# Channels 0 to 3 and 4 to 7 on the two partition halves, and how half two's first inverse is evacuated

## The chip, the cores and the metric

The kernel runs on one core of a Trainium2 chip. The metric is the device time of one execution in microseconds (us). Engines are named as in the profile: PE multiplies matrices (PEld is its weight load), ACT, DVE and POOL work elementwise, SP issues most transfers. PSUM is the memory that PE writes, 8 banks of 512 float32 columns on 128 partitions; SBUF is the memory that everything else is kept in.

## The reference, cut to what matters

The input is a sequence of 2048 tokens with 512 channels. Two layers follow one another, and each is a long convolution with a gate, then an MLP:

```python
def _A_ref(q, k, v, shift_k, ssm_k, ssm_D):
    # a causal convolution of four taps over k, times v
    kv = k_shift * v
    kv_f = rfft(kv padded to 2 * S)          # along the sequence, for each channel
    kf_f = rfft(ssm_k padded to 2 * S)
    y = irfft(kv_f * kf_f)[:S]               # a causal convolution as long as the sequence
    y = y + kv * ssm_D
    return q * y

def _B_ref(x, w1, b1, w2, b2):
    h = gelu(layernorm(x) @ w1 + b1)
    return h @ w2 + b2

x = A_q
x = x + _A_ref(layernorm(x), A_k, A_v, A_shift_k, A_ssm_k, A_ssm_D)
x = x + _B_ref(layernorm(x), B_w1, B_b1, B_w2, B_b2)
# and the same two lines once more, with the same A_k, A_v, A_ssm_k and weights
```

Since k, v and the filter are the same in both layers, the convolution's result y is computed once and used twice.

## The kernel before, in words

The sequence is cut into two halves of 1024 tokens. The output of half one needs the convolution of half one's input with half one of the filter. That of half two needs two products, which are added in the frequency domain. Each convolution is a transform in two stages, a product, and an inverse in two stages, all by matmuls:

- `stage1` (PE on line 557) transforms along 128 points, for eight groups of eight channels in one PSUM tile of two banks. Its evacuation (line 560) reads, for each of 128 places, eight elements 128 columns apart, and writes 1024 in a row.
- `stage2` (PE on line 569) transforms along the remaining 8 points with the table S2. Its output has on the partitions 8 channels of a group x 8 frequencies x real and imaginary part, and the order of the channels there is the order of S2's columns. In the kernel before, the even channels 0, 2, 4, 6 are on partitions 0 to 63 and the odd ones on 64 to 127. Its evacuation reads the tile as `[512,2],[32,16],[1,32]` (step and count, outermost first) and, for the input's transforms (line 730 for half one, line 788 for half two), writes `[32,2],[64,16],[1,32]`.
- `inverse1` (PE on line 674) inverts the 8 points with the table U. For half one (`split` false) a group of eight channels takes two matmuls of 128 rows and 128 columns, and the evacuation (lines 681 and 682) reads `[8,16],[128,8],[1,8]` and writes `[512,16],[8,8],[1,8]`. For half two (`split` true) each group takes, for each half of the partitions (`g` 0 and 1), two matmuls of 64 rows and 64 columns. Half `g` writes bank `g` of the tile: 16 blocks of 32 columns, four channels for each of eight groups in a block. Since U does not mix channels, only the columns of the four channels of that half are taken from it. The evacuation of such a tile (lines 678 and 679) is the one that the change edits. There are eight tiles.
- `inverse2` (PE on line 696) inverts the 128 points, and needs the evacuations of all eight tiles of `inverse1`. Its result is y, with the tokens on the partitions.

`evac` on line 473 is ACT's copy out of PSUM (line 474 is DVE's), so all these evacuations have the same line in the profile. `tt` on line 468 is DVE's elementwise operation.

After that come blocks of one to four tiles of 128 tokens, for each half and layer: statistics (lines 810 to 825), normalisation (835 on ACT, 836 on DVE), times y and added, statistics again and normalisation, a transpose (on PE, or by a DMA on line 879), the first MLP matmul (`m1`, PE on line 899, with the GELU on ACT, line 904), and the second (`m2`, PE on line 933, added by DVE on line 937).

The order of all operations over all engines is written out by hand (`SEQ`), and so is the engine of each operation that could run on ACT, DVE or POOL (`ENGS`) and the PSUM banks of each tile (`BANKS`). Neither reads the data or the layout. From the order, `arrange` and `sync` work out which waits are needed; an engine runs its own list strictly in order. Around the edited place PE has the eight `inverse1` groups of half two interleaved with MLP matmuls of half one: three groups, one more, six `m2` matmuls, four groups, eleven `m2` matmuls, and then `inverse2`. The eight tiles share three pairs of banks, in PE's order 2, 4, 6, 2, 4, 2, 6, 4 (the first bank of each pair), so a group waits until the earlier tile in its banks has been evacuated. All eight evacuations are on ACT, one behind the other, in the order of the groups except that the third and the fourth change places; behind them stands a normalisation (line 835) of a later block.

Of the kernel before, what the change touches and what calls it, by code (L numbers as in the profile page):

```python
# [349 lines left out]
def _tables():  # L350

    be = np.arange(128)[:, None]
    k1 = 2 * np.arange(128)[None, :]
    th = TWO_PI * be * (k1 + 0.5) / 256
    F = np.concatenate([np.cos(th), -np.sin(th)], 1)
    a = np.arange(8)
    k2 = np.arange(8)
    f = 2 * np.arange(128)[:, None] + 0.5 + 256 * k2[None, :]
    th = TWO_PI * a[:, None, None] * f[None] / 2048
    c, s = np.cos(th), np.sin(th)  # L360
    S2 = np.zeros((2, 8, 8, 128, 2, 8, 8))
    for d in range(8):
        S2[0, :, d, :, 0, :, d] = c
        S2[1, :, d, :, 0, :, d] = s
        S2[0, :, d, :, 1, :, d] = -s
        S2[1, :, d, :, 1, :, d] = c
    S2 = S2[..., [0, 2, 4, 6, 1, 3, 5, 7]].transpose(0, 1, 2, 3, 6, 5, 4).reshape(128, 128 * 128)
    ph = TWO_PI * k2[:, None] * a[None, :] / 8
    c, s = np.cos(ph), np.sin(ph)
    U = np.zeros((2, 8, 8, 2, 8, 2, 8))  # L370
    for d in range(8):
        U[0, :, d, 0, :, 0, d] = c
        U[1, :, d, 0, :, 0, d] = -c
        U[0, :, d, 0, :, 1, d] = s
        U[1, :, d, 0, :, 1, d] = -s
        U[0, :, d, 1, :, 0, d] = -s
        U[1, :, d, 1, :, 0, d] = -s
        U[0, :, d, 1, :, 1, d] = c
        U[1, :, d, 1, :, 1, d] = c
    U = U[:, :, [0, 2, 4, 6, 1, 3, 5, 7]].transpose(2, 1, 0, 3, 4, 5, 6).reshape(128, 256)  # L380
    t = 8 * np.arange(128)[None, :] + a[:, None]
    ps = TWO_PI * t[None] * (2 * np.arange(128)[:, None, None] + 0.5) / 2048
    T2 = np.stack([np.cos(ps), -np.sin(ps)], 2) / 1024
    T2 = T2.reshape(128, 2048)
    sg = np.where(np.arange(128)[:, None] % 2 == 0, -1.0, 1.0) * np.ones((1, 16))
    return F, S2, U, T2, sg

# [5 lines left out]
def bass_interleave_layers__ssm_conv_h3__mixer_channel_mlp__prompt_kernel(  # L393
# [7 lines left out]
    def A(p0, n, off, *dims):  # L401
        return bass.AP(ar, p0 * AR + off, [[AR, n]] + [list(d) for d in dims])
# [7 lines left out]
    def Q(tile, p0, n, off, *dims):  # L410
        return bass.AP(ps, p0 * 4096 + tile.base * 512 + off, [[4096, n]] + [list(d) for d in dims])
# [12 lines left out]
    def place(n):  # L424
        o = pos[0]
        pos[0] += -(-n // 16) * 16
        return o

    R_ID, R_F, R_SG, R_B1 = place(192), place(256), place(16), place(16)
    R_U, R_DG, R_TC, R_HALO = place(256), place(1024), place(16), place(16)  # L430
# [15 lines left out]
    assert M_SG + 1 <= NS  # L446

    F, S2, U, T2, sg = _tables()
    t_sm = nc.inline_tensor(_bf(np.concatenate([np.eye(128), np.eye(128)[:, :64] + np.eye(128)[:, 64:], F, sg, U, T2], 1)), name="tab_small")
    t_s2 = nc.inline_tensor(_bf(S2), name="tab_s2")  # L450
# [19 lines left out]
    def evac(engs, dst, src, durs, tile):  # L470
        def f(e):
            if e is nc.scalar:
                return e.activation(dst, src(), AF.Copy)  # L473
            return e.tensor_copy(dst, src())  # L474
        return P.op(engs, f, durs, writes=[dst], tile=tile)

    BOTH = (ACT, DVE)
    E1 = {ACT: 912.0, DVE: 1135.0}
# [28 lines left out]
    tl = Tile(2)  # L507
# [7 lines left out]
    tl = Tile(1)  # L515
# [8 lines left out]
    for i in range(4):  # L524
        o, t = A(0, 128, R_DG + i * 256, [64, 4], [1, 64]), A(0, 128, R_TC + 4 * i, [1, 4], [0, 64])
# [36 lines left out]
    def stage2(G, t):  # L562

        tl = Tile(2)
        ins = [(i, A(0, 128, R_S2 + (16 * t + i) * 128, [1, 128]), A(0, 128, G + (16 * t + i) * 8, [1024, 8], [1, 8])) for i in range(16)]

        def f(e):
            for i, w, m in ins:
                r = e.matmul(Q(tl, 0, 128, i // 8 * 512 + i % 8 * 4, [32, 16], [1, 4]), w, m, start=True, stop=True)  # L569
            return r  # L570
        P.op(PE, f, 16 * 30.0, reads=[x for y in ins for x in y[1:]], tile=tl)
        return tl
# [81 lines left out]
    def hap(r, t, d, g=None):  # L654
        return A(0, 128, r + 64 * t + (4096 * g if g else 0), [d, 2], [512, 16 if g is None else 8], [1, 64])

    def inverse1(p, q, Z, split):

        for j in range(8):
            tl = Tile(2)  # L660
            ins = []
            for i in range(8):
                dg = 8 * j + i
                for n, r in enumerate((p, q)):
                    o = r + (dg // 4) * 512 + dg % 4
                    if split:
                        for g in range(2):
                            ins.append((512 * g + 4 * i, n, A(64 * g, 64, o, [4, 128]), A(64 * g, 64, R_U + n * 128 + g, [8, 16], [2, 4])))
                    else:
                        ins.append((i * 128, n, A(0, 128, o, [4, 128]), A(0, 128, R_U + n * 128, [1, 128])))  # L670

            def f(e, ins=ins, tl=tl):
                for i, n, w, m in ins:
                    r = e.matmul(Q(tl, 0, 128, i, *([32, 16], [1, 4]) if split else ([1, 128],)), w, m, start=n == 0, stop=n == 1)  # L674
                return r
            P.op(PE, f, 32 * 18.0 if split else 16 * 56.0, reads=[x for y in ins for x in y[2:]], tile=tl)
            if split:
                evac(BOTH, A(0, 128, Z + 64 * j, [1, 2], [512, 16], [2, 32]),
                     lambda tl=tl: Q(tl, 0, 128, 0, [512, 2], [32, 16], [1, 32]), E1, tl)
                continue  # L680
            evac(BOTH, A(0, 128, Z + 64 * j, [512, 16], [8, 8], [1, 8]),
                 lambda tl=tl: Q(tl, 0, 128, 0, [8, 16], [128, 8], [1, 8]), E1, tl)
# [25 lines left out]
    for t in range(8):  # L708
        tl = stage2(R_2, t)
# [17 lines left out]
    for t in range(8):  # L727
        tl = stage2(R_3, t)
# [24 lines left out]

    P.tag = "i1_0"
    inverse1(R_1, R_2, R_3, False)
    P.tag = "i2_0"
    inverse2(R_3, R_YT[0])

    P.tag = "h2_1"
    for t in range(8):  # L760
        tl = stage2(R_G1, t)
        for g in range(2):
            w = 64 * t + 32 * g
            o, x = A(0, 128, R_3 + w, [512, 16], [1, 32]), A(0, 128, HI + w, [512, 16], [1, 32])
# [7 lines left out]
    for t in range(8):  # L772
        o = hap(R_3, t, D1)
# [10 lines left out]
    for t in range(8):  # L784
        P.tag = "x2_1"
        tl = stage2(R_6, t)
        xo = R_KT + 1024 * (t % 4)
        evac(BOTH, A(0, 128, xo, [32, 2], [64, 16], [1, 32]), lambda tl=tl: Q(tl, 0, 128, 0, [512, 2], [32, 16], [1, 32]), E1, tl)
        o, p = hap(HH, t, HI - HH), hap(R_3, t, D1)
        tt(o, A(0, 128, xo, [0, 2], [64, 16], [1, 64]), o, ALU.mult, 1137.0)  # L790
        P.tag = "sum"
        tt(o, o, p, ALU.add, 1137.0)
    P.tag = "i1_1"
    inverse1(HH, HI, R_Z1, True)
    P.tag = "i2_1"
    inverse2(R_Z1, R_YT[1])
# [50 lines left out]
    for half in range(2):  # L847
        HTS, XTS, W = R_HT[half], R_XT[half], (256, 512)[half]
        for i in range(2):
            o = A(96, 1, HTS[i] + 10 * W, [1, W])  # L850
            P.op(POOL, lambda e, o=o: e.memset(o, 1.0), 100.0 + W, writes=[o])
        for L in range(2):
            s0 = 0
            for n in BLOCKS[half][L]:
# [18 lines left out]
                for i, (xo, yo) in enumerate(sl):  # L873
# [8 lines left out]
                    tl = Tile(1)  # L882
# [9 lines left out]
                for fc in range(11):  # L892
                    rows = 128 if fc < 10 else 96
                    tl = Tile(1)
                    ins = [(A(0, 128, R_W1 + dk * 1376 + fc * 128, [1, rows]), A(0, 128, XTS[k] + dk * W, [1, w])) for dk in range(4)]
# [11 lines left out]
                for i, (xo, yo) in enumerate(sl):  # L907
                    P.tag = "m2"
                    s = ids[i]
                    tl = Tile(1)  # L910
                    ins = []
# [62 lines left out]
```

## Time and profile before

| | us |
|---|---|
| median of 3 runs | 240.69 |
| lowest and highest | 240.51, 241.71 |
| the profiled execution | 240.1 |
| its span, first to last instruction | 238.2 |
| PE, DVE, ACT busy | 223.9, 176.6, 163.5 |

A row of a timeline gives the start from the beginning of the span, the time that the row lasts, the engine, the line, the operation with its shapes and how many instructions are in it, and in brackets the idle time ahead of it with what ended it. A row of the chain of work that ended last gives the start, the time and what that time belongs to. A row of a line's own view gives the shortest, the median and the longest duration in ns, and the first and the last start. A row of busy times by stretches gives the stretch, its length, the busy time of each engine with its instructions, the granted clock and the share of DMA.

### The profile page before, as it was taken

What the parts mean: (1) busy time and instruction counts of PE and PEld (TensorE: products, weight loads), DVE (VectorE), ACT (ScalarE), POOL (GpSimd) and SP (SyncE); (2) the same over time, 40 slices, a digit from 0 to 9 for tenths busy, and PEclk for the clock granted to TensorE, in tenths of its full rate; (3) what the DMA queues carried; (4) which work ended last, traced back from release to release, by engine and by line L of the source; (5) the groups of instructions that cost most, each with busy time, mean ns of one, the idle gap of its engine ahead of it and who ended that gap; (6) DMA issues with size and microseconds to landing.
All of it is one profiled execution on the core that took longest, in us unless ns stands there. A gap on an engine that the chain in (4) does not pass through costs nothing.

```text
span 238.2 us, 6507 instructions
## 1 busy us (share of the span) xinstructions
PE 223.9 (94%) x2743; PEld 147.7 (62%) x2765; DVE 176.6 (74%) x353; ACT 163.5 (69%) x258; POOL 57.0 (24%) x122
## 2 busy tenths in 40 slices
PE   6998788998999999998997999999999999999995
PEld 2897577876868587666866474844444444444453
DVE  0479989999999999999999599783269577605013
ACT  2485889999886779998969998477017415752540
POOL 2421030316412229177004232203020302300000
PEclk9999999999999999999999999999999999999999
DMA  5999789979959240022500203501300050033002
GB/s 158 360 387 388 279 219 196 304 237 174 165 121 277 51 91 3 1 47 49 174 0 6 44 4 66 154 3 22 66 1 3 0 132 0 0 69 117 37 3 88
DMA packets 41113, 26.77 MB, mean 112 GB/s; under 512 B 23702, under 2 KB 33788, under 8 KB 41084
## 3 DMA queue, kind: packets, MB, share of 16 engines
q1 hardware_dynamic: 40786, 26.20, 40.9%
q8 instruction: 22, 0.36, 0.6%
q10 hardware_dynamic: 298, 0.16, 0.3%
q14 instruction: 7, 0.06, 0.1%
HBM read 15.07 MB, written 2.10 MB: 72 GB/s over the span
## 4 chain that ended last, share of the span: by engine, by line
PE 64%; ACT 15%; DVE 9%; POOL 5%; DMA 4%; issue 2%; SPq 1%; DVEq 0%; ACTq 0%
PE ps L899 28%; PE ps L933 24%; ACT ar L473 13%; DVE ar L468 3%; PE ps L557 3%; POOL sm L825 3%; DMA ar<-in_A_ssm_k_dram 3%; PE ps L674 2%; DVE sm L810 2%; DMA ar<-ar 2%; ACT ar L835 2%; PE ps L696 2%; DVE ar L620 1%; PE ps L922 1%; PE ps L642 1%
## 5 line engine op out<-in xcount | busy, mean ns | idle before, releaser
L904 ACT ACTIVATE ar<-ps,sm 128x256 bf16<-128x256 f32 (+5 forms) x143 | 65.1, 525 | 36.3 <-PE ps L899 35.8
L473 ACT ACTIVATE ar<-ps 128x1024 bf16<-128x1024 f32 (+3 forms) x77 | 73.1, 1039 | 14.2 <-PE ps L557 5.9
L899 PE MATMUL ps<-ar 128*128 128x256 bf16 (+5 forms) x568 | 80.4, 297 | 0.3
L933 PE MATMUL ps<-ar 128*128 128x512 bf16 (+1 forms) x324 | 75.9, 380 | 1.4 <-issue 0.8
L899 PEld LDWEIGHTS ps<-ar 128*128 128x128 bf16 (+1 forms) x572 | 52.5, 100 | 27.3 <-ACT ar L473 0.4
L468 DVE TENSOR_TENSOR ar<-ar 128x512 bf16<-128x512 bf16 (+3 forms) x105 | 62.9, 637 | 6.1 <-ACT ar L835 5.5
L933 PEld LDWEIGHTS ps<-ar 128*128 128x128 bf16 (+1 forms) x341 | 32.1, 98 | 35.5 <-ACT ar L904 0.6
L810 DVE BATCH_NORM_STATS2 sm<-ar 128x6 f32<-128x512 bf16 x64 | 42.5, 682 | 0.4
L835 ACT ACTIVATE ar<-ar,sm 128x512 bf16<-128x512 bf16 x37 | 28.4, 811 | 12.7 <-DVE sm L822 7.5
L815 POOL TENSOR_SCALAR sm<-sm 128x2 f32<-128x2 f32 (+2 forms) x23 | 7.4, 323 | 106.1 <-DVE sm L811 105.6
L937 DVE TENSOR_TENSOR ar<-ar,ps 128x512 bf16<-128x512 bf16 x31 | 20.5, 677 | 16.0 <-PE ps L933 16.0
L817 POOL TENSOR_TENSOR sm<-sm 128x2 f32<-128x2 f32 (+2 forms) x26 | 22.1, 851 | 18.5 <-DVE sm L815 16.6
L557 PE MATMUL ps<-ar 128*64 128x128 bf16 x512 | 18.4, 227 | 2.8 <-ACT ar L473 1.1
L569 PE MATMUL ps<-ar 128*128 128x64 bf16 x512 | 18.3, 194 | 1.2 <-ACT ar L473 1.0
L557 PEld LDWEIGHTS ps<-ar 128*64 128x64 bf16 x512 | 15.8, 115 | 5.6 <-issue 2.1
L569 PEld LDWEIGHTS ps<-ar 128*128 128x128 bf16 x512 | 16.9, 98 | 3.8 <-ACT ar L473 2.0
L825 POOL TENSOR_SCALAR sm<-sm 128x1 f32<-128x1 f32 x43 | 17.6, 424 | 2.0
L836 DVE TENSOR_SCALAR ar<-ar,sm 128x512 bf16<-128x512 bf16 x27 | 10.7, 407 | 7.5 <-POOL sm L825 7.3
L474 DVE CAST ar<-ps 128x1024 bf16<-128x1024 f32 x11 | 13.1, 1220 | 3.2 <-PE ps L569 1.9
L674 PE MATMUL ps<-ar 64*128 64x64 bf16 (+1 forms) x384 | 12.6, 203 | 1.5 <-ACT ar L473 1.1
L674 PEld LDWEIGHTS ps<-ar 64*128 64x128 bf16 (+1 forms) x384 | 11.9, 114 | 2.8 <-ACT ar L473 1.4
L474 DVE COPY ar<-ps 128x1024 bf16<-128x1024 bf16 (+1 forms) x9 | 5.5, 632 | 8.1 <-PE ps L520 5.4
(41 smaller groups left out, 94.1 us busy)
## 6 DMA issues: line engine op xcount, KB each, us to landing
ar<-tab_s SPq DMA_DIRECT2D x16, 256.0 KB, 9.3
ar<-ar SPq DMA_DIRECT2D x16, 256.0 KB, 3.9
ar<-in_A_ssm_k_dram SPq DMA_DIRECT2D x8, 256.0 KB, 6.7
ar<-in_A_q_dram SPq DMA_DIRECT2D x8, 256.0 KB, 4.3
ar<-in_A_v_dram SPq DMA_DIRECT2D x8, 256.0 KB, 6.6
out_dram<-ar SPq DMA_DIRECT2D x7, 256.0 KB, 2.5
ar<-in_B_w_dram SPq DMA_DIRECT2D x4, 344.0 KB, 4.4
ar<-in_B_w_dram SPq DMA_DIRECT2D x5, 256.0 KB, 4.7
```

What stands on the lines that cost most here:

```text
L468: return P.op(eng, lambda e: e.tensor_tensor(o, a, b, op), dur, reads=[a, b] + list(more), writes=[o])
L473: return e.activation(dst, src(), AF.Copy)
L557: r = e.matmul(Q(tl, 64 * ri, 64, i * 128, [1, 128]), w, m, start=True, stop=True)
L569: r = e.matmul(Q(tl, 0, 128, i // 8 * 512 + i % 8 * 4, [32, 16], [1, 4]), w, m, start=True, stop=True)
L674: r = e.matmul(Q(tl, 0, 128, i, *([32, 16], [1, 4]) if split else ([1, 128],)), w, m, start=n == 0, stop=n == 1)
L810: P.op(DVE, lambda e, sj=sj, x=x: e.bn_stats(sj, x), 600.0, reads=[x], writes=[sj])
L817: P.op(POOL, lambda e: e.tensor_tensor(r, v, hf, ALU.pow), 420.0 + 149.0 * n, reads=[v, hf], writes=[r])
L825: o = e.tensor_scalar(x, y, z, -1.0, ALU.mult, ALU.mult)
L835: return e.activation(o, x, AF.Identity, bias=u, scale=r)
L899: r = e.matmul(Q(tl, 0, rows, 0, [1, w]), a, m, start=dk == 0, stop=dk == 3)
L904: P.op(ACT, lambda e, dst=dst, tl=tl, rows=rows, bias=bias, w=w: e.activation(dst, Q(tl, 0, rows, 0, [1, w]), AF.Gelu_apprx_tanh, bias=bia ...
L933: r = e.matmul(Q(tl, 0, 128, 0, [1, 512]), ins[fc][0], ins[fc][1], start=fc == 0, stop=fc == 10)
```

## The change

The channels of a group lie on the partitions in their own order: 0 to 3 on partitions 0 to 63 and 4 to 7 on 64 to 127. To that end the columns of S2 and the rows of U are no longer permuted. In the first inverse of half two, the slice of U for partition half `g` is then four neighbouring columns of each block of eight, from column `4 * g`, instead of every other column from column `g`.

In the evacuated tile the four channels of half `g` are the channels `4 * g` to `4 * g + 3` of each group. The evacuation therefore reads, for each of 16 blocks and each of eight groups, four columns from the first bank and four from the second, and writes 64 elements in a row. Before, it read all of the first bank in runs of 32 columns and then the second, and wrote each of them to every other element. Everything else, the order, the engines, the banks and the transfers, is as it was.

```diff
@@ _tables
-    S2 = S2[..., [0, 2, 4, 6, 1, 3, 5, 7]].transpose(0, 1, 2, 3, 6, 5, 4).reshape(128, 128 * 128)
+    S2 = S2.transpose(0, 1, 2, 3, 6, 5, 4).reshape(128, 128 * 128)
...
-    U = U[:, :, [0, 2, 4, 6, 1, 3, 5, 7]].transpose(2, 1, 0, 3, 4, 5, 6).reshape(128, 256)
+    U = U.transpose(2, 1, 0, 3, 4, 5, 6).reshape(128, 256)
@@ inverse1
                     if split:
                         for g in range(2):
-                            ins.append((512 * g + 4 * i, n, A(64 * g, 64, o, [4, 128]), A(64 * g, 64, R_U + n * 128 + g, [8, 16], [2, 4])))
+                            ins.append((512 * g + 4 * i, n, A(64 * g, 64, o, [4, 128]), A(64 * g, 64, R_U + n * 128 + 4 * g, [8, 16], [1, 4])))
...
             if split:
-                evac(BOTH, A(0, 128, Z + 64 * j, [1, 2], [512, 16], [2, 32]),
-                     lambda tl=tl: Q(tl, 0, 128, 0, [512, 2], [32, 16], [1, 32]), E1, tl)
+                evac(BOTH, A(0, 128, Z + 64 * j, [512, 16], [1, 64]),
+                     lambda tl=tl: Q(tl, 0, 128, 0, [32, 16], [4, 8], [512, 2], [1, 4]), E1, tl)
                 continue
```

## The prediction

> **What bounds the kernel now.** I read the head of the page, then the chain of work that ended last, then the busy time by stretches around the edited stage, then the timelines of the engines in that stage.
>
> ```profile
> span 238.2 us, 6507 instructions
> PE 223.9 (94%) x2743; PEld 147.7 (62%) x2765; DVE 176.6 (74%) x353; ACT 163.5 (69%) x258; POOL 57.0 (24%) x122
> ```
> ```profile
> 124.17 0.67 PE ps L674 x32
> 124.85 0.02 issue
> 124.87 9.59 ACT ar L473 x8
> 134.45 0.04 issue
> 134.50 2.33 PE ps L696 x10
> ...
> 154.96 0.05 issue
> 155.01 9.44 PE ps L899 x43
> ```
> ```profile
> core 0: us, PE busy (x) PEld busy (x) DVE busy (x) ACT busy (x) POOL busy (x), PEclk, DMA share, GB/s
> 124.10:134.50 10.40, 8.72 (x273) 6.17 (x274) 8.04 (x23) 9.63 (x9) 4.24 (x10) 1.00 0.14 28
> 134.50:155.00 20.50, 20.41 (x136) 13.41 (x139) 17.59 (x48) 15.36 (x29) 5.12 (x9) 1.00 0.27 66
> 155.00:199.00 44.00, 43.78 (x200) 20.09 (x204) 27.23 (x69) 19.58 (x33) 6.56 (x15) 1.00 0.14 30
> ```
> PE is the bound of the whole, but not here. The edited stage is the one place late in the span where the chain leaves PE: from 124.87 to 134.45 it runs through eight evacuations on ACT (L473), the first inverse of half two (its matmuls are L674). ACT is busy 9.63 of the 10.40 us, PE 8.72. After 134.50 PE is busy 20.41 of 20.50 and 43.78 of 44.00, at full clock: what PE is ahead at 134.50 it can keep, if its inputs come ahead too.
>
> **The odd row.** The eight, and their durations against those of half two's second forward transform (the same tile and the same number of elements):
>
> ```profile
> 124.87 9.57 ACT L473 ACTIVATE ar<-ps 128x1024 bf16<-128x1024 f32 x8 [1.54 <-PE ps L674]
> 134.19 0.89 ACT L835 ACTIVATE ar<-ar,sm 128x512 bf16<-128x512 bf16 x1
> 135.57 1.94 ACT L473 ACTIVATE ar<-ps 128x1024 bf16<-128x1024 f32 x2 [0.50 <-PE ps L696]
> ```
> ```profile
> L473 ACT ACTIVATE ar<-ps x8: 1311/1378/1399, 124.9 to 133.1; 128x1024 bf16<-128x1024 f32 x8
> ...
> L473 ACT ACTIVATE ar<-ps x8: 1002/1027/1049, 101.9 to 111.6; 128x1024 bf16<-128x1024 f32 x8
> ```
> ```profile
> 11.25 2.85 ACT L473 ACTIVATE ar<-ps 128x1024 bf16<-128x1024 f32 x3 [0.36 <-PE ps L557]
> ...
> 47.58 3.77 ACT L473 ACTIVATE ar<-ps 128x1024 bf16<-128x1024 f32 x4 [0.34 <-PE ps L674]
> ...
> 109.80 2.83 ACT L473 ACTIVATE ar<-ps 128x1024 bf16<-128x1024 f32 x3
> ```
> Neighbouring evacuations overlap, so I use the step from start to start, (run minus the last one's duration) over (count minus one). The eight: (9.57 - 1.39)/7 = 1.17 us. The others: (2.85 - 1.03)/2 = 0.91, (3.77 - 1.04)/3 = 0.91, (2.83 - 1.02)/2 = 0.905. The row at 109.80 is the second forward transform, whose evacuation reads PSUM by exactly the pattern of the old one in the edited place ([512,2],[32,16],[1,32]) and writes whole runs of 32. The only difference to the slow eight is the destination: [1,2],[512,16],[2,32], every other bf16 element. So I put the 0.265 us (1.17 - 0.905) down to the write with step 2.
>
> **The change, part by part.** (1) The two tables, the slice of U and its step: the same bytes and the same DMAs; channels change partitions and nothing else moves. Cost 0. (2) The moving operand of the L674 matmuls of half two has step 1 instead of 2. No row of before shows this pair apart. Lower bound 0 gain; upper bound from these rows:
>
> ```profile
> 109.19 0.63 PE L569 MATMUL ps<-ar 128*128 128x64 bf16 x16
> ...
> 131.00 0.72 PE L674 MATMUL ps<-ar 64*128 64x64 bf16 x32 [0.47 <-ACT ar L473]
> ```
> Sixteen matmuls of 64 contiguous columns take 0.63 us, sixteen pairs of 64 stepped columns 0.72: at most 0.09 a group, and 4 groups lie on the path below, so 0.36 us. I take 0, the pairs being a different form. (3) The evacuation: written in runs of 64 (as the first inverse of half one, the row at 47.58, 0.91), read in runs of four columns from two banks in turn. The nearest read is stage 1's (row at 11.25, 0.91): eight elements 128 columns apart, so four from one bank and four from the next, in turn. Bounds of the new step: 0.905, by those rows, and 1.17, if the step of the write is not the cause. I take 0.905, as both halves of the new pattern have a row of their own at that value. Not the other engine: the plan's letters put all eight on ACT, and the row x8 shows it.
>
> The Trainium skill, page "SBUF — State Buffer", section "Door 1", box on cachelines, speaks against this: SBUF lines are 16 bytes, two hits on a line give full rate, so a bf16 step up to 8 elements is free. By it a step of 2 costs nothing, the 1.17 has another cause, and the change would bring nothing; it is rival 1's reading. The two rows that differ in the destination alone (1.17 and 0.905) disagree with it.
>
> **The sum.** 8 x 0.265 = 2.1 us is what ACT saves, but PE's own work and the banks' order cut it. PE's rows of before:
>
> ```profile
> 124.11 1.79 PE L674 MATMUL ps<-ar 64*128 64x64 bf16 x96
> 126.27 0.72 PE L674 MATMUL ps<-ar 64*128 64x64 bf16 x32 [0.37 <-ACT ar L473]
> 127.14 1.25 PE L933 MATMUL ps<-ar 128*128 128x512 bf16 x5 [0.16 <-issue]
> 128.33 1.25 PE L674 MATMUL ps<-ar 64*128 64x64 bf16 x64
> 129.81 0.72 PE L674 MATMUL ps<-ar 64*128 64x64 bf16 x32 [0.23 <-ACT ar L473]
> 131.00 0.72 PE L674 MATMUL ps<-ar 64*128 64x64 bf16 x32 [0.47 <-ACT ar L473]
> 131.88 2.32 PE L933 MATMUL ps<-ar 128*128 128x512 bf16 x10 [0.16 <-issue]
> 134.50 2.33 PE L696 MATMUL ps<-ar 128*128 128x512 bf16 x10 [0.29 <-ACT ar L473]
> ```
> Name PE's groups P1 to P8 and the evacuations E1 to E8 in ACT's order. Three groups are issued at once (P1 to P3, banks 2, 4, 6); P4 waits for E1 (bank 2), P5 for E2 (4), P6 for E3 (2), P7 for E4 (6), P8 for E5 (4); MLP matmuls stand between P4 and P5 and after P8; E3 needs P4, E5 P5, E6 P6, E7 P7, E8 P8. A group is issued in about 0.54 us ((1.79 - 0.19)/3), its evacuation can start 0.76 after its start (124.87 - 124.11), PE restarts 0.06 after an evacuation's end (126.27 against 124.87 + 1.34). New, with a duration of 1.02 to 1.03 and the step 0.905:
> - E1 124.87 to 125.89; P4 starts 125.95 (was 126.27); E2 to 126.81; E3 finds P4 just through at 126.71.
> - P5 stands 2.06 behind P4 (128.33 - 126.27, MLP between): 128.01. E2 is long done.
> - E5 cannot start before P5 is through: 128.01 + 0.76 = 128.77, though ACT is free at 128.52. Here the gain is cut once. E5 ends 129.79.
> - P6 and P7 follow P5 without a wait (128.56, 129.10). P8 waits for E5: 129.85 (was 131.00).
> - The MLP matmuls follow P8 by 0.88 (131.88 - 131.00) and last to 134.21 (134.50 less its wait of 0.29), that is 2.33: now 130.73 to 133.06.
> - E6, E7, E8 end 130.71, 131.62, 132.53: before 133.06. L696, which waited for E8, now waits for nothing but PE's own order, and starts at 133.06 instead of 134.50.
>
> The gain at that point is 1.44 us. The row of stretches bounds it from above: PE was idle 10.40 - 8.72 = 1.68 us there. What was late on other queues moves too: the normalisation L835 of the next block stands right behind E8 on ACT (134.19), so it starts at about 132.4, and DVE, which waits for it, starts sooner:
>
> ```profile
> 130.76 0.59 POOL L825 TENSOR_SCALAR sm<-sm 128x1 f32<-128x1 f32 x2
> ...
> 135.10 1.22 DVE L468 TENSOR_TENSOR ar<-ar 128x512 bf16<-128x512 bf16 x3 [2.74 <-ACT ar L835]
> ```
> L835's input from POOL is there at 131.35, so it holds nothing back; DVE gets ahead by about 1.8. Does PE keep 1.44? The nearest input that comes by another way is the transposed block of four tiles for the m1 matmuls at 155.01:
>
> ```profile
> 142.30 9.57 SPq L879 DMA_TRANSPOSE ar<-ar  x6
> ...
> DMA to landing us min/median/max: 2.4/2.4/2.5
> ```
> The last of these transposes, 1.27 long, is issued at 150.6 and lands at about 153.1. Even if nothing of the DVE and ACT work ahead of it moved, PE would want it at 155.01 - 1.44 = 153.57: in time by 0.5. It does move, since DVE is ahead. SP issues them one behind the other, so they go as their inputs go. After that PE paces its own inputs. I take all of the 1.44 to the end.
>
> The profiled execution took 240.1 us in all (its span of 238.2 and 1.9 around it): 240.1 - 1.44 = 238.7. The median of the runs shown, 240.69, is 0.59 above that execution; for a median I forecast 240.69 - 1.44 = 239.2.
>
> **The rivals.**
> 1. *The write's step is not the cause*, and the eight stay at 1.17: no gain, 240.7 as a median. (By the rule of the Trainium skill above this is the outcome.) What would be the cause then is something of the stage, such as matmuls on 64 rows that write two banks at once. Against it:
> ```profile
> 79.55 1.12 PE L642 MATMUL ps<-ar 32*128 32x128 bf16 x88
> ...
> 79.91 1.02 ACT L473 ACTIVATE ar<-ps 128x1024 bf16<-128x1024 f32 x1 [0.67 <-DVE ar L468]
> ```
> An evacuation that lies wholly beside matmuls on 32-row groups takes 1.02.
> 2. *The gain is only partly kept*: a wait further on, or PE's order, leaves 0.2 to 1.2 us of it: 239.5 to 240.5. Against it the 0.5 us of room and PE's full stretches; for it that 1.44 is only just above what a measurement can tell from nothing (0.5%, 1.2 us).
> 3. *Slower: each change of bank costs ACT time.* The new read changes bank 256 times in 1024 elements. One element takes 0.905/1024 = 0.88 ns. With two lost a change, the step is 0.905 + 256 x 1.77 ns = 1.36, and eight of them add 8 x (1.36 - 1.17) = 1.5 us on the path: 242.2. It decides from 1.04 ns a change (0.265/256), where the gain of the write is used up, and is slower by 0.5% from a step of 1.32. Against it stage 1's row: the same 256 changes, 0.91.
> 4. *More than forecast*: the matmuls gain too (up to 0.36). ACT allows E8's end at 132.53, so L696 at 132.59 at the earliest: at most 0.5 us more, 238.7.
>
> **How the numbers follow.** Forecast, with rival 4 in it: 0.62. Rival 2: 0.18. Rival 1: 0.11. Rival 3: 0.09. Faster by over 0.5%: 0.62; within: 0.29; slower: 0.09. The likeliest time is 239.2, its own range 238.3 to 239.6 (rival 4 at 238.7, less 0.4, about the distance between runs; 0.4 above). To leave out no more than 2 in 10 the range must reach over rivals 2 and 1: 238.3 to 240.9.
>
> **What would show it.** Right: the eight L473 at a step near 0.905 and durations near 1.03 instead of 1.38; L696 released by PE's own order, with no wait for ACT ahead of it, at about 133.1; PE as busy as before after that; everything later by about 1.4 us sooner. A new short wait of ACT for L674 ahead of the fifth evacuation (about 0.25 us). Wrong: a step still at 1.17 (rival 1) or above (rival 3); or an early L696 and a wait for a transpose or for ACT before the m1 matmuls at 153.6 (rival 2). What I cannot see in the trace of before is the write with step 1 and the read by fours in one instruction.

## The result, and the profile after

The changed kernel takes 238.75 us (median of 20 runs, 236.84 to 240.18), the kernel before 240.51 (median of 20 runs beside them, 239.06 to 241.71). The ratio is 0.9927, with a 95% interval of 0.9906 to 0.9947: 1.3 to 2.3 us less. The profiled execution took 238.15 us, with a span of 236.3.

The chain of work that ended last, in order of time:

```profile
123.84 0.67 PE ps L674 x32
124.52 0.02 issue
124.54 1.03 ACT ar L473
...
128.44 1.03 ACT ar L473
129.47 0.05 issue
129.52 0.72 PE ps L674 x31
130.24 0.16 issue
130.40 2.32 PE ps L933 x10
132.72 2.16 PE ps L696 x10
```

The chain no longer runs through all eight evacuations. It touches ACT at two of them, the first (124.54) and the fifth (128.44), and otherwise stays on PE. L696 follows the MLP matmuls L933 with nothing between.

The evacuations' own view (shortest, median and longest in ns) and who waited for them:

```profile
L473 ACT ACTIVATE ar<-ps x8: 1018/1023/1046, 124.5 to 131.2; 128x1024 bf16<-128x1024 f32 x8
...
who waited for it (us, times):
  PEld ps L674: 0.7, 3
```

1378 ns have become 1023. ACT's other copies of this size and these types take 1001 to 1156 ns in the kernel before, 1030 in the median. L696, which used to wait, is gone from the list. PE's timeline, start and duration:

```profile
123.78 2.56 PE L674 MATMUL ps<-ar 64*128 64x64 bf16 x128
126.50 1.25 PE L933 MATMUL ps<-ar 128*128 128x512 bf16 x5 [0.16 <-issue]
127.68 2.56 PE L674 MATMUL ps<-ar 64*128 64x64 bf16 x128
130.40 2.32 PE L933 MATMUL ps<-ar 128*128 128x512 bf16 x10 [0.16 <-issue]
132.56 2.32 PE L696 MATMUL ps<-ar 128*128 128x512 bf16 x10
```

From the first group of the first inverse (L674) to the second inverse (L696) it is now 132.56 - 123.78 = 8.78 us; it was 134.50 - 124.11 = 10.39. I call this the length of the stage from here on. It is 1.61 us shorter. The other 0.33 us between the two traces lie ahead of the stage (it starts at 123.78 and not at 124.11), where the change puts the channels in another order and alters no instruction.

The busy time by stretches:

```profile
123.77:132.56 8.79, 8.36 (x272) 6.18 (x274) 8.04 (x23) 7.89 (x9) 3.61 (x10) 1.00 0.09 19
132.56:153.06 20.50, 20.40 (x137) 13.41 (x138) 17.59 (x48) 15.13 (x29) 5.74 (x10) 1.00 0.30 72
153.06:197.05 43.99, 43.78 (x200) 20.11 (x204) 27.23 (x69) 19.55 (x33) 6.56 (x15) 1.00 0.14 30
```

In the stage PE is busy 8.36 of 8.79 us, and ACT 7.89. Two matmuls are missing from these records (L933 shows 5 and 10 where the kernel has six and eleven), so PE is busier than this row says; the next trace has them all. It is PE's stage now, with the two evacuations of the chain left in it. The stretches behind it are as long as they were, 20.50 and 43.99 against 20.50 and 44.00, so the gain is handed on whole. From L696 to the end it is 236.3 - 132.56 = 103.7 us, and it was 238.2 - 134.50 = 103.7.

The inputs of the later matmuls come sooner too. The rows of DVE behind L835 and of the transposes:

```profile
132.94 1.22 DVE L468 TENSOR_TENSOR ar<-ar 128x512 bf16<-128x512 bf16 x3 [0.90 <-ACT ar L835]
...
140.13 9.57 SPq L879 DMA_TRANSPOSE ar<-ar  x6
```

Counted from the start of the stage, DVE's row comes at 9.16 us in place of 10.99, and the transposes at 16.35 in place of 18.19: both 1.8 us sooner.

### The profile page after: what moved, and what is told of

Read it like the earlier page. It is cut to its first block, busy times and chain, and to the rows that moved or that the text cites. A ratio compares the mean times of both kernels' runs of the same rounds, so it can differ in the third digit from the quotient of the medians.

```text
span 236.3 us, 6507 instructions
## 1 busy us (share of the span) xinstructions
PE 223.0 (94%) x2743; PEld 147.4 (62%) x2765; DVE 176.6 (75%) x353; ACT 161.4 (68%) x258; POOL 55.9 (24%) x122
## 4 chain that ended last, share of the span: by engine, by line
PE 67%; DVE 11%; ACT 9%; DMA 6%; POOL 3%; issue 2%; SPq 1%; DVEq 0%; ACTq 0%; POOLq 0%
PE ps L899 28%; PE ps L933 25%; ACT ar L473 7%; DVE ar L468 5%; PE ps L674 4%; DMA ar<-ar 4%; PE ps L557 4%; DMA ar<-in_A_ssm_k_dram 2%; DVE sm L810 2%; POOL sm L825 2%; DVE ar L620 1%; PE ps L696 1%; ACT ar L835 1%; PE ps L922 1%; DVE ar L651 1%
## 5 line engine op out<-in xcount | busy, mean ns | idle before, releaser
L473 ACT ACTIVATE ar<-ps 128x1024 bf16<-128x1024 f32 (+3 forms) x77 | 71.1, 1004 | 13.8 <-PE ps L557 6.0
L933 PE MATMUL ps<-ar 128*128 128x512 bf16 (+1 forms) x324 | 75.8, 379 | 1.4 <-issue 0.6
L933 PEld LDWEIGHTS ps<-ar 128*128 128x128 bf16 (+1 forms) x341 | 32.2, 98 | 35.5 <-ACT ar L904 0.6
L835 ACT ACTIVATE ar<-ar,sm 128x512 bf16<-128x512 bf16 x37 | 28.4, 809 | 11.8 <-DVE sm L822 7.1
L674 PEld LDWEIGHTS ps<-ar 64*128 64x128 bf16 (+1 forms) x384 | 11.8, 114 | 1.8 <-DVE ar L468 1.0
L674 PE MATMUL ps<-ar 64*128 64x64 bf16 (+1 forms) x384 | 12.4, 203 | 0.5 <-DVE ar L468 0.4
```

What stands on the lines that cost most here:

```text
L835: return e.activation(o, x, AF.Identity, bias=u, scale=r)
L933: r = e.matmul(Q(tl, 0, 128, 0, [1, 512]), ins[fc][0], ins[fc][1], start=fc == 0, stop=fc == 10)
```

## The experiments

The theory: a write to every other bf16 element is what made the eight evacuations slow; with that gone PE's own order sets the stage, and the rest of the program moves with it. The rivals: the layout or the moving operand of the matmuls brings the gain; the read, with its changes of bank, costs or gains something; the stage and not the write made ACT slow; the gain between the medians is partly chance.

### The changed kernel once more

> The changed kernel once more, as the yardstick of this group. In its first trace PE's first L674 group of half two starts 8.79 us ahead of L696 (10.39 in the kernel before), so 1.6 us shorter. Theory (the write with step 2 is what cost, PE's order cuts the gain): the same 8.8 us, evacuations of 1.02 us, and a time 1.4 to 1.8 us under the kernel before. Rival (most of the 1.76 us between the medians is chance): under 1 us.

Measured: 238.87 us, ratio 0.9921 (0.9892 to 0.9949). Against 240.77 for the kernel before in this group that is 1.90 us less (1.2 to 2.6), a little more than the 1.4 to 1.8 of the theory and not the rival's under 1. The trace:

```profile
125.13 2.56 PE L674 MATMUL ps<-ar 64*128 64x64 bf16 x128
...
133.91 2.32 PE L696 MATMUL ps<-ar 128*128 128x512 bf16 x10
```
```profile
125.12:133.91 8.79, 8.68 (x274) 6.18 (x274) 8.04 (x23) 7.90 (x9) 3.62 (x10) 1.00 0.09 19
```

With all matmuls recorded PE is busy 8.68 of the 8.79 us. The stage is 8.78 us again, although it starts 1.35 us later in the span than in the first trace. What varies between the traces here lies ahead of the stage, so the stage's length is a sharper measure of this change than the time of the whole: two traces agree within 0.01 us, the whole span differs by 1.3 (237.6 against 236.3).

### The write alone

The kernel before, with its own layout, tables and slices; only the evacuation's order is another, one column from each bank in turn, so that it writes runs.

```diff
-                evac(BOTH, A(0, 128, Z + 64 * j, [1, 2], [512, 16], [2, 32]),
-                     lambda tl=tl: Q(tl, 0, 128, 0, [512, 2], [32, 16], [1, 32]), E1, tl)
+                evac(BOTH, A(0, 128, Z + 64 * j, [512, 16], [1, 64]),
+                     lambda tl=tl: Q(tl, 0, 128, 0, [1, 512], [512, 2]), E1, tl)
```

> The kernel before with its even and odd channels and its slices of U, but the evacuation written in runs of 64, read with a change of bank at every column (1024 changes in place of 1 before and 256 in the changed kernel). Theory of the write: evacuations of 1.02 us with a step near 0.905, the stage 8.8 us long, and the time of the changed kernel (about 1.6 us under before), though no channel has moved. Rival, that a change of bank costs: a step above 0.905, by up to four times what the changed kernel lost to it. Rival, that the new layout of channels or the moving operand brings the gain: a stage of 10.4 us and no gain.

Measured: 238.75 us, ratio 0.9929 (0.9897 to 0.9960). The evacuations' view, and PE's timeline:

```profile
L473 ACT ACTIVATE ar<-ps x8: 1017/1024/1042, 126.6 to 133.2; 128x1024 bf16<-128x1024 f32 x8
```
```profile
125.83 2.56 PE L674 MATMUL ps<-ar 64*128 64x64 bf16 x128
...
134.62 2.32 PE L696 MATMUL ps<-ar 128*128 128x512 bf16 x10
```

The stage is 8.79 us. The whole gain is there, with no channel moved and the moving operand still at step 2. So the new layout is not needed for it, and the step of the moving operand is worth nothing here. Nor does a change of bank cost ACT anything: with 1024 of them, one at each element, the evacuation takes the same 1024 ns.

### The step alone put back

The changed kernel, with its layout and its read in runs of four, but every other element written.

```diff
-                evac(BOTH, A(0, 128, Z + 64 * j, [512, 16], [1, 64]),
+                evac(BOTH, A(0, 128, Z + 64 * j, [1, 2], [512, 16], [2, 32]),
```

> The changed kernel with its new layout and its new read in runs of four, but written to every other element again, as before (the channels of y lie in another order, so the output is another). Theory of the write: the step goes back to 1.17, the stage to 10.4 us, and the time to that of the kernel before (0 to 0.3 us off). Rival, that the layout or the read brings the gain: it stays at 0.905 and 8.8.

Measured: 240.91 us, ratio 1.0007 (0.9983 to 1.0030).

```profile
L473 ACT ACTIVATE ar<-ps x8: 1315/1371/1392, 124.8 to 133.0; 128x1024 bf16<-128x1024 f32 x8
```
```profile
124.00 1.78 PE L674 MATMUL ps<-ar 64*128 64x64 bf16 x96
126.16 0.72 PE L674 MATMUL ps<-ar 64*128 64x64 bf16 x32 [0.37 <-ACT ar L473]
...
134.40 1.90 PE L696 MATMUL ps<-ar 128*128 128x512 bf16 x8 [0.29 <-ACT ar L473]
```

The kernel before is back: the durations (1371 ns, and 1378 there), the waits of PE, a stage of 10.40 us (10.39 there) and the time (0.14 us off). This run differs from the changed kernel in the pattern of the write alone; the run above also reads in another order. Together they settle the cause: the step of the write, and nothing else of the change, makes the difference.

### The same write in another stage

```diff
-        x = A(0, 128, HX + 1024 * t, [32, 2], [64, 16], [1, 32])
+        x = A(0, 128, HX + 1024 * t, [1, 2], [64, 16], [2, 32])
...
-        evac(BOTH, A(0, 128, xo, [32, 2], [64, 16], [1, 32]), lambda tl=tl: Q(tl, 0, 128, 0, [512, 2], [32, 16], [1, 32]), E1, tl)
+        evac(BOTH, A(0, 128, xo, [1, 2], [64, 16], [2, 32]), lambda tl=tl: Q(tl, 0, 128, 0, [512, 2], [32, 16], [1, 32]), E1, tl)
```

> The changed kernel with the write to every other element in another stage: the evacuations of the input's second forward transform in both halves (eight tiles each, some of half one's on DVE), where the matmuls have 128 rows. The channels of the input's transform then lie in another order, so the output is another. Theory of the write: wherever ACT writes with step 2 it takes 1.31 to 1.40 us, with a step of 1.17, against 1.00 to 1.07 and 0.905 in these places before; the first inverse of half two stays at 1.02. Rival, that the stage made it slow: 1.00 to 1.07 here too. DVE's (1.22 us contiguous) I have no row for: unchanged if DVE's own rate is the limit.

Measured: 242.37 us in one execution. The evacuations of half two's second forward transform (the first row), those of the first inverse of half two (the second), and three of DVE's in half one (the third):

```profile
L473 ACT ACTIVATE ar<-ps x8: 1303/1316/1328, 104.6 to 115.2; 128x1024 bf16<-128x1024 f32 x8
...
L473 ACT ACTIVATE ar<-ps x8: 1018/1023/1046, 128.7 to 135.3; 128x1024 bf16<-128x1024 f32 x8
...
L474 DVE CAST ar<-ps x3: 1224/1321/1330, 32.7 to 36.4; 128x1024 bf16<-128x1024 f32 x3
```

The slowness goes where the write with step 2 goes: the forward transform takes 1316 ns in place of 1027, and 1.15 to 1.18 us from start to start where its copies stand back to back, beside matmuls of 128 rows, while the first inverse is quick. The stage is not the cause. DVE pays too, but less: its two evacuations with step 2 take 1321 and 1330 ns; the first of the row, which the edit does not touch, takes 1224.

### Other steps

```diff
-                evac(BOTH, A(0, 128, Z + 64 * j, [512, 16], [1, 64]),
-                     lambda tl=tl: Q(tl, 0, 128, 0, [32, 16], [4, 8], [512, 2], [1, 4]), E1, tl)
+                evac(BOTH, A(0, 128, Z + 64 * j, [1, (16, 8, 4, 16, 8, 4, 4, 8)[j]], [512, 16], [(16, 8, 4, 16, 8, 4, 4, 8)[j], 64 // (16, 8, 4, 16, 8, 4, 4, 8)[j]]),
+                     lambda tl=tl: Q(tl, 0, 128, 0, [512, 2], [1, 512]), E1, tl)
```

> The changed kernel, the eight evacuations read in PSUM's order and written with other steps (the channels of y lie in another order, so the output is another). In ACT's order: the first three step 4 elements (8 bytes), the next three step 8 (16 bytes), the last two step 16 (32 bytes). If each element that does not share a 4-byte word with the one before it costs the same, all stay at a step of about 1.17 us and durations of 1.31 to 1.40. If it goes by lines of 16 bytes, two hits at full rate, step 4 is as quick as a run (0.905) and steps 8 and 16 are slower than 1.17. If it grows with the step, 4 is above 1.17 and 16 the slowest.

Measured: 261.8 us in one execution. Steps of 4, 8 and 16 elements, in this order:

```profile
125.18 7.07 ACT L473 ACTIVATE ar<-ps 128x1024 bf16<-128x1024 f32 x3 [1.54 <-PE ps L674]
...
131.99 13.89 ACT L473 ACTIVATE ar<-ps 128x1024 bf16<-128x1024 f32 x3
...
145.37 9.04 ACT L473 ACTIVATE ar<-ps 128x1024 bf16<-128x1024 f32 x2
```

From start to start: (129.69 - 125.18)/2 = 2.25 us at step 4, (140.81 - 131.99)/2 = 4.41 at step 8, and 149.66 - 145.37 = 4.29 at step 16. With 0.905 for a run and 1.17 at step 2, the time about doubles with each doubling of the step from 4 to 16 bytes, and at 32 bytes (a single pair of copies) it is no longer. None of the three readings that I had written down fits all of it: it grows with the step, but 16 is not slower than 8.

PE's timeline begins and ends with:

```profile
124.42 1.79 PE L674 MATMUL ps<-ar 64*128 64x64 bf16 x96
...
154.46 1.89 PE L696 MATMUL ps<-ar 128*128 128x512 bf16 x4 [8.63 <-ACT ar L473]
```

PE's stage is then 154.46 - 124.42 = 30.0 us long, and the time is 21 us above that of the kernel before. The stage makes 19.6 of them: the price on ACT is again the price on the path. Behind L696 it is 105.4 us in place of 103.7, at a granted clock of 0.98 where it was 1.00.

### Runs of four, half of each 16 bytes

Each evacuation in two instructions, one for each bank.

```diff
-                evac(BOTH, A(0, 128, Z + 64 * j, [512, 16], [1, 64]),
-                     lambda tl=tl: Q(tl, 0, 128, 0, [32, 16], [4, 8], [512, 2], [1, 4]), E1, tl)
+                P.op(BOTH, lambda e, d=[A(0, 128, Z + 64 * j + 4 * g, [512, 16], [8, 8], [1, 4]) for g in range(2)], tl=tl: [e.activation(d[g], Q(tl, 0, 128, 512 * g, [1, 512]), AF.Copy) for g in range(2)][1],
+                     E1, writes=[A(0, 128, Z + 64 * j, [512, 16], [1, 64])], tile=tl)
```

> The changed kernel, each evacuation as two instructions, one for each bank, written in runs of four elements (8 bytes) with a gap of four. The values are those of the changed kernel. If what costs is each visit to a 16-byte piece of SBUF, about 4.5 ns (1.17 us / 256 visits, 2.3 / 512, 4.4 / 1024), then 128 visits of an instruction take 0.57 us and a pair 1.15 to 1.2 from start to start. If whole 4-byte words are written at full rate, a pair takes about 0.95 (two steps of the 512-element copies, some 0.48 each).

Measured: 238.53 us in one execution.

```profile
L678 ACT ACTIVATE ar<-ps x16: 593/622/671, 124.9 to 132.2; 128x512 bf16<-128x512 f32 x16
```

From start to start it is 0.48 us, and 0.96 for a pair (single records of the trace). Two plain copies of 512 elements, written in a row, stand in the trace of the kernel before, 1.08 - 0.59 = 0.49 us apart:

```profile
52.26 1.08 ACT L473 ACTIVATE ar<-ps 128x512 bf16<-128x512 f32 x2
```

So the visits to 16-byte pieces are not what is paid for: there are as many of them as with step 2, and the copy is as quick as a plain one. My 4.5 ns for a visit falls.

### Runs of two, and wider gaps

```diff
-                evac(BOTH, A(0, 128, Z + 64 * j, [512, 16], [1, 64]),
-                     lambda tl=tl: Q(tl, 0, 128, 0, [32, 16], [4, 8], [512, 2], [1, 4]), E1, tl)
+                u, v = ((4, 16), (2, 8), (1, 2), (4, 16), (1, 2), (2, 4), (2, 4), (2, 8))[j]
+                m = 1024 * u // v
+                P.op(BOTH, lambda e, d=[A(0, 128, Z + 64 * j + u * g, [512, 16], [v, 64 // v], *([[1, u]] if u > 1 else [])) for g in range(v // u)], tl=tl, m=m: [e.activation(x, Q(tl, 0, 128, m * g, [1, m]), AF.Copy) for g, x in enumerate(d)][-1],
+                     E1, writes=[A(0, 128, Z + 64 * j, [512, 16], [1, 64])], tile=tl)
```

> The changed kernel, each evacuation in several instructions with other patterns of the write (the channels of y lie in another order, so the output is another). In ACT's order: two evacuations in runs of 2 elements, every 4 elements (2 x 512 elements); two in single elements, every 2 (2 x 512); two in runs of 2, every 8 (4 x 256); two in runs of 4, every 16 (4 x 256). If only a lone element that leaves half of its 4-byte word costs extra, everything but the second pair runs at full rate: 0.48 us from start to start for 512 elements (as runs of four did), some 0.26 for 256; the second pair 0.58 to 0.61. If it goes by visits to 16-byte pieces at 4.4 ns, the runs of 2 every 8 take 128 visits, 0.56 us for 256 elements, and the runs of 4 every 16 take 64, 0.28.

Measured: 240.26 us in one execution. In order: runs of 2 every 4, single elements every 2, runs of 2 every 8, runs of 4 every 16:

```profile
125.65 2.07 ACT L680 ACTIVATE ar<-ps 128x512 bf16<-128x512 f32 x4 [1.55 <-PE ps L674]
...
127.57 2.59 ACT L680 ACTIVATE ar<-ps 128x512 bf16<-128x512 f32 x4
...
129.94 2.45 ACT L680 ACTIVATE ar<-ps 128x256 bf16<-128x256 f32 x8
...
132.09 2.51 ACT L680 ACTIVATE ar<-ps 128x256 bf16<-128x256 f32 x8
```

From the first start of a group to the next group's: 1.92/4 = 0.48 us for runs of 2, 2.37/4 = 0.59 for single elements, 2.15/8 = 0.27 for runs of 2 that are 16 bytes apart, and within the last group 0.26 for runs of 4 that are 32 bytes apart. Pairs of 512 elements run at the rate of the plain copy (0.49), and single elements of the same size do not. For 256 elements no trace has a plain copy; carried on from 0.905 and 0.48, my estimate for one is 0.27, which the pairs that are 16 bytes apart keep to as well. That fits the reading by words. Each pair lies on a 4-byte word of its own here, and pairs across two words were not tried, so it is not shown whether the word counts or merely that an element is written next to the one before it.

### PE's order changed

The gain was cut by PE's order, so I tried one with fewer waits: three of the six MLP matmuls between the groups go ahead of the fourth group, the other three behind the fifth. The evacuations of the third and the fourth group come in the groups' order.

```diff
-        360, 757, 682, 361, 801, 686, 365, 800, 759, 370, 758, 760, 358, 683, 371, 761, 762, 356, 802, 858, 359, 362,
-        803, 856, 763, 735, 357, 766, 804, 861, 857, 767, 859, 736, 764, 363, 862, 805, 737, 806, 765, 809, 863, 807,
+        682, 360, 757, 365, 801, 370, 361, 686, 800, 759, 356, 371, 758, 760, 358, 683, 357, 761, 762, 362, 802, 858,
+        359, 803, 856, 763, 735, 766, 804, 861, 857, 767, 859, 736, 764, 363, 862, 805, 737, 806, 765, 809, 863, 807,
```

> The changed kernel with another order in the stage: three of the six MLP matmuls stand ahead of the fourth group of the first inverse, the other three behind the fifth, and the evacuations of the third and fourth groups come in the groups' order. If PE's waits for banks (about 0.2 us ahead of the fourth and 0.25 ahead of the eighth group) are what is left between PE and its own work, the stage is 8.78 - 0.25 = 8.5 us long, and at most 0.45 shorter; the time is 0.1 to 0.4 us under the changed kernel, which these rounds can hardly tell apart. If ACT is still the limit, it stays at 8.8.

Measured: 238.99 us, ratio to the kernel before 0.9944 (0.9910 to 0.9977), which cannot be told from the changed kernel's. PE's timeline:

```profile
126.06 1.78 PE L674 MATMUL ps<-ar 64*128 64x64 bf16 x96
127.78 0.82 PE L933 MATMUL ps<-ar 128*128 128x512 bf16 x3
128.53 1.38 PE L674 MATMUL ps<-ar 64*128 64x64 bf16 x64
129.85 0.82 PE L933 MATMUL ps<-ar 128*128 128x512 bf16 x3
130.60 1.79 PE L674 MATMUL ps<-ar 64*128 64x64 bf16 x96
132.33 2.55 PE L933 MATMUL ps<-ar 128*128 128x512 bf16 x11
134.72 2.32 PE L696 MATMUL ps<-ar 128*128 128x512 bf16 x10
```

PE's rows show no idle time any more, and the stage is 8.66 us, 0.12 shorter, half of what I expected. How much of the 8.66 is PE's own work, no run here separates, since the recorded end of a matmul is late (below). It is no version that can be shown to beat the changed kernel.

## Why the prediction was right

- **The odd row and its cause.** Right. The step of the write was picked out by comparing two rows that differ in the destination, but also in the stage that they stand in, so before the runs it was an argument. Three runs make it a finding: the step put back (the write's pattern alone is edited), the write alone (with the order of the read that it needs), and the same write in another stage.
- **The new step of 0.905.** Right: 0.903 to 0.92 wherever ACT does not wait.
- **Tables, slices and layout at 0.** Right. The moving operand, for which I kept up to 0.36 us, is worth nothing: with step 1 and step 2 the stage is 8.78 and 8.79 us.
- **The walk through PE's order.** In us after the start of the first group, forecast and single records of the trace: fourth group 1.84 and 1.84; fifth 3.90 and 3.90; fifth evacuation 4.66 and 4.66 (the forecast wait of ACT, 0.25, is there: a step of 1.15); eighth group 5.74 and 5.74; MLP matmuls behind it 6.62 and 6.62; end of the eighth evacuation 8.42 and 8.44.
- **L696.** Forecast at 8.95, measured at 8.78. Here one term was off: I let the MLP matmuls last 2.33 us, to the end of the last one less L696's wait in the row (0.29). In the new trace L696 starts 2.16 after them (132.56 - 130.40). A matmul's end stands later in the records than the moment when PE takes the next, by 0.17 us here, so the old wait of L696 was 0.46 and not 0.29. That is all of the difference between 1.44 and 1.61. For the same reason my bound of 1.68 from the idle time in the stretch is none, though that idle time even holds two MLP matmuls that are missing from the records: the reordered stage is 10.39 - 8.66 = 1.73 us shorter.
- **All of it to the end.** Right. From L696 to the end it is 103.7 us in the kernel before, in the changed kernel, in its second trace (237.6 - 133.91) and with the step put back (238.1 - 134.40). The DVE row behind L835 and the transposes are 1.8 us sooner, as forecast, and PE waits for neither.
- **The time.** 239.2 was forecast, 238.75 measured, from a median of before that lies 0.18 lower in the larger set of runs. A gain of 1.44 was forecast, 1.76 measured (1.3 to 2.3), of which the stage shows 1.61; the 0.15 left is within the interval. So the 0.5 us between 239.2 and 238.75 are the lower median (0.18), the mis-sized wait (0.17) and this rest.
- **The rivals.** Rival 1 (not the write) and rival 3 (changes of bank) fall by the experiments, rival 2 by the 103.7 us. Rival 4's mechanism, a gain of the matmuls, was not there; that its time of 238.7 is nearly the measured one is chance, by the terms just named.

The rule of the Trainium skill that I weighed, page "SBUF — State Buffer", section "Door 1" (lines of 16 bytes, two hits on a line at full rate, so a step of up to 8 bf16 free), does not hold for ACT's writes here. Steps 2 and 4 put four and two elements on such a piece and cost 0.27 and 1.35 us for 1024 elements. Sixteen bytes do show up, though: of the steps measured it is the one from which the cost no longer grows.

## What to carry to other kernels

Where ACT copies float32 results out of PSUM as bf16, let it write at least two neighbouring elements at a time, on one 4-byte word, and put the gather on the PSUM side, where an odd order cost nothing in any run here, down to a change of bank at each element. Look for such a copy by its duration, the same line, shape and engine at 1.38 us in one stage and about 1.03 in the others, and make sure by the time from start to start: recorded durations reach 1.16 us in a long row of quick copies that still start 0.90 apart. Then walk the bank order by hand, group by group, since of the 2.1 us that ACT saved PE's order let 1.6 through; and take the time from one start to the next, not the recorded end of a matmul.

## What the runs showed of the hardware that I had not expected

The price of writing single bf16 elements on ACT, from start to start for 1024 elements: 0.905 us in a run, 1.17 at a step of 4 bytes, 2.25 at 8, 4.41 at 16 and 4.29 at 32. Pairs at a pitch of 8 bytes and runs of four at 16 take 0.48 for 512 elements, as a plain copy does (0.49); pairs at 16 and runs of four at 32 take 0.26 to 0.27 for 256. So it hangs on whether an element is written together with its neighbour. Whether the two must share a 4-byte word, and why the price of a lone one grows with the step, up to 16 bytes, no run here tells. DVE's copy pays much less for step 2: 1.32 in place of 1.22 us.
